# Second stage of a routed two-layer block: rows gathered two experts ahead, whole tiles for large experts, small experts as one chain

## The chip, the cores and the metric

The kernel runs on one core of a Trainium2 chip. The metric is the device time of one execution in microseconds (us), lower is better. Engines are named as in the profile: PE is TensorE's matmul, PEld its weight load, DVE VectorE, ACT ScalarE, POOL GpSimd, SP SyncE. The names with a q behind them (PEldq, POOLq) are the sequencers of these engines: branches, semaphores and the issue of DMAs. L12 is line 12 of the kernel.

## The reference

Three parts follow one another. An attention with rotated queries and keys (4 batches, 8 heads, 576 positions, 64 wide) gives 2304 token rows of 512. A gated layer makes `x = (silu(x @ w_gate) * (x @ w_val)) @ w_out` of them (1536 wide). The third part is a routed layer of 8 experts:

```
do_compute = x @ w_skip > 0                # a token that does not compute keeps its row
xc     = x[do_compute]
logits = xc @ w_gate
e_idx  = argmax(logits)                    # one expert for each token
gate_w = softmax(logits)[e_idx]
y[e]   = gate_w * (relu(xc[e] @ w1[e]) @ w2[e])        # w1: 512x1024, w2: 1024x512
out    = x, and xc + y for the tokens that compute
```

How many rows an expert gets depends on the data; with the inputs used it is 299, 35, 55, 544, 28, 14, 322 and 1 for experts 0 to 7.

## The kernel before

The first two parts end at about 843 us of the span; the change touches what comes then. While the second part runs, each chunk of 384 tokens is routed as soon as it is finished: `note` (L771) writes, for each token that computes, its number, its place in the output and its gate into a list of its expert in a table in DRAM. Expert 0 starts before the last chunk is routed; its first list entries are raised to 128 (`close_first`, L774), which leaves holes, so that its list ends at 335.

`first` runs expert 0's first tile (x00) between the last pieces of the second part, builds the lists of its next two tiles by matmuls (`compare`, `late_list`), gathers their rows (x01, x02), then notes the last chunk and sorts experts 1 to 7 (`sort`): those with more than 64 tokens first. `counts` loads the sorted counts and expert numbers from SBUF into registers of the engines. From here on "expert 1" is the first in the sorted order; here the order is 544, 322, 35, 55, 28, 14, 1.

`run` then loads the index lists (ix, L1367, six tiles of 128 entries for each expert) and the weights. A ring of 21 raw tiles of 512 KB holds weights, eight tiles for an expert (four of w1, four of w2); `w_more(e)` loads what follows when expert e is done. SP issues all of these in program order. POOL issues gathers (L1108) and stores (L1191, L1223); both are indirect DMAs.

An expert with more than 64 rows ("large") is computed in tiles of 128 rows. `ffn` does one: `up` twice (L1141, L1144, one for each half of the 1024 wide middle layer), `turn` twice (L1198, transposes), `down` (L1214 to L1217), `store`. Weights and rows are each split in a high and a low part (eh by ACT at L1071, el by DVE at L1072; `half`), so that each product is three matmuls at a fast rate. The splitting of an expert's weights stands inside its first tile. `mid` transposes the rows of the next tile (`x_T`, L1116) between the two turns. `more` nests the tiles: an `If` per further tile (L1433), each of which gathers the rows of the tile after next.

What is left of an expert behind its whole tiles and is up to 64 rows ("the rest") goes through `few_up`, `few_turn`, `few_down` (L1158 and following), in an `If` of its own: `rest` loads its part of the list (ixrest, L1352, on ACT's queue), `rest_gather` its rows (rest_rows). So a tile starts whole when more than 64 rows are left.

An expert with up to 64 rows ("small") goes through `raw_ffn` in an `If` of its own (L1387), five of these in a row here: gather the next expert's rows, rH for both halves (L1257, the raw weights without a split), the next expert's rows transposed (xTf, L1127), rhT (L1268), Y (L1272), store, `w_more`.

`hint` places a hint of a coming branch on TensorE's sequencer.

Of the kernel before, what the change touches and what calls it, by code (L numbers as in the profile page):

```python
# [7 lines left out]
F32 = mybir.dt.float32  # L8
# [490 lines left out]
class Moe1:  # L499
# [258 lines left out]
    def placed(self, c):  # L758
        nc, k = self.nc, self.k
        pos, row, ps = self.r.pop(c)  # L760
        nc.vector.tensor_tensor(k["run"], k["run"], ps[:, TT * E:(TT + 1) * E], op=ALU.add)
        posu = self.p2.tile([P, TT], U32, tag="rposu", name=f"rposu_{c}")
        nc.vector.tensor_copy(posu, pos)
        self.r[c] = pos, row, posu

# [59 lines left out]
    def sort(self):  # L825
# [17 lines left out]
        nc.vector.tensor_copy(k["n"][0:1, 1:E], pos)  # L843
        nc.vector.tensor_copy(k["n"][0:1, 0:1], nf[:, 0:1])
        nc.vector.tensor_tensor(t, m, col(desc), op=ALU.mult)
        nc.vector.tensor_reduce(pos, t, axis=AX.X, op=ALU.add)
        nc.vector.tensor_scalar(k["n"][0:1, E:], pos, -1.0, float(E), op0=ALU.mult, op1=ALU.add)

    def counts(self):
        load = self.nc.values_load_multi_w_load_instructions  # L850
        n = load(self.k["n"][0:1, 0:E], min_val=0, max_val=NTOK)[1]
        ids = load(self.k["n"][0:1, E:], engines=[mybir.EngineType.SP, mybir.EngineType.Activation], min_val=1, max_val=E - 1)[1]
        return n[0], n[1:], ids
# [83 lines left out]
def load_consts(nc, lasting, c, w, tok, cf, w_gate, w_skip, table):  # L937
# [16 lines left out]
    k["n"] = lasting.tile([P, 2 * E - 1], I32, tag="n", name="n")  # L954
# [24 lines left out]
class Moe2:  # L979
# [4 lines left out]
    def __init__(self, tc, c, w, px, w1, w2, x2d, table, out, ident):  # L984
        self.tc, self.nc, self.w, self.c, self.px = tc, tc.nc, w, c, px
        self.w1, self.w2, self.x2d, self.table, self.out, self.ident = w1, w2, x2d, table, out, ident
        self.W = {}
        self.ring = None
        self.n, self.place, self.pair, self.both = {}, {}, {}, {}
        self.raws = []  # L990
# [9 lines left out]
    def open(self, ctx):  # L1000
        self.fold = self.c.tile([P, FEW], F32, tag="fold", name="fold")
        self.nc.vector.tensor_reduce(self.fold, self.ident.rearrange("p (c a) -> p c a", a=2), axis=AX.X, op=ALU.add)
        self.p1 = ctx.enter_context(self.tc.tile_pool(name="e_1", bufs=1))
        self.fold2 = self.p1.tile([P, FEW], F32, tag="fold2", name="fold2")
        self.nc.vector.tensor_tensor(self.fold2, self.ident[:, :FEW], self.ident[:, FEW:], op=ALU.add)
        self.raws += [self.w.ring.tile([P, F2], I32, tag="raw", name=f"wr{i}") for i in range(4)]
        self.raws.append(self.p1.tile([P, F2], I32, tag="raw2", name="wr4"))
        self.rest_rows = self.p1.tile([P, DM], F32, tag="rest_rows", name="rest_rows")
        self.xf = [self.p1.tile([P, 4 * FEW], F32, tag=f"xf{i}", name=f"xf{i}") for i in range(2)]
        self.xrest = self.p1.tile([P, 2 * DM], F32R, tag="xrest", name="xrest")  # L1010
# [140 lines left out]
    def few_up(self, e, x, fh, work=()):  # L1151

        nc = self.nc
        ps = self.bank("H", f"H{fh}")
        for kt in range(KT):
            for i, w in enumerate(self.w1_of(e, kt, fh)):
                nc.tensor.matmul(ps, x["hl"][:, 2 * kt * P:(2 * kt + 1) * P], w, start=(kt + i == 0),  # L1158
                                 stop=(kt == KT - 1 and i == 1))
        for f in work:  # L1160
            f()
        h = self.w.tmp.tile([P, 512], F32, tag="y2", name=f"h{fh}")
        nc.scalar.copy(h, ps)
        return h

    def few_turn(self, fh, h):

        nc = self.nc
        ps = self.bank("U", f"hT{fh}")[:, :4 * FEW]
        for i in range(4):  # L1170
            nc.tensor.matmul(ps[:, i * FEW:(i + 1) * FEW], h[:, i * P:(i + 1) * P], self.fold, start=True, stop=True)
        ps = ps.rearrange("p (i c) -> p i c", i=4)
        th, tl = self.both[1 - fh][:, :4 * P].rearrange("p (i a c) -> a p i c", i=4, a=2)
        nc.scalar.activation(th, ps, AF.Relu)
        nc.vector.scalar_tensor_tensor(tl, ps, 0.0, f32(th), op0=ALU.max, op1=ALU.subtract)

    def few_down(self, e):
        nc = self.nc
        self.y = self.bank("Y", "Y")
        for n in range(8):  # L1180
            for i, w in enumerate(self.W[1][n // 4]):
                nc.tensor.matmul(self.y, self.both[1 - n // 4][:, n % 4 * P:(n % 4 + 1) * P], w[:, n % 4, :],
                                 start=(n + i == 0), stop=(n == 7 and i == 1))

# [41 lines left out]
    def ffn(self, x, mid=None, few=False, split=None, end=None):  # L1226

        up, turn, down, store = (getattr(self, "few_" * few + f) for f in ("up", "turn", "down", "store"))
# [6 lines left out]
        h0 = up(0, x, 0)  # L1235
        rows(range(0, 3))
        h1 = up(0, x, 1)
        turn(0, h0)
# [3 lines left out]
        turn(1, h1)  # L1242
        rows(range(5, 8))
        if end:
            end()
        down(0)
        store(x)

    def raw_ffn(self, e, x, mid):

        nc = self.nc
        side = lambda ps, a: ps[a * FEW:(a + 1) * FEW]
        hs = []
        for fh in range(2):
            ps = self.bank("H", f"rH{fh}")
            for kt in range(KT):
                nc.tensor.matmul(side(ps, kt % 2), x["f"][:, kt * FEW:(kt + 1) * FEW],  # L1257
                                 self.w.raw[e, kt][:, fh * 512:(fh + 1) * 512],
                                 start=(kt < 2), stop=(kt >= 2), skip_group_check=True)
            h = self.w.tmp.tile([P, 512], F32, tag="y2", name=f"rh{fh}")  # L1260
            nc.scalar.copy(h, ps)
            hs.append(h)
        mid()
        hT = self.w.tmp.tile([P, 8 * FEW], F32, tag="f", name="rhT")
        for fh in range(2):
            ps = self.bank("U", f"rhT{fh}")[:, :4 * FEW]
            for i in range(4):
                nc.tensor.matmul(ps[:, i * FEW:(i + 1) * FEW], hs[fh][:, i * P:(i + 1) * P], self.fold2, start=True, stop=True)  # L1268
            nc.scalar.activation(hT[:, fh * 4 * FEW:(fh + 1) * 4 * FEW], ps, AF.Relu)
        self.y = self.bank("Y", "Y")  # L1270
        for n in range(8):
            nc.tensor.matmul(side(self.y, n % 2), hT[:, n * FEW:(n + 1) * FEW],  # L1272
                             self.w.raw[e, KT + n // 2][:, n % 2 * 512:(n % 2 + 1) * 512],
                             start=(n < 2), stop=(n >= 6), skip_group_check=True)
        self.few_store(x)
# [31 lines left out]
    def first(self):  # L1307
# [40 lines left out]
    def rest(self, base, n, eng):  # L1348

        at = ((n + (P - FEW - 1)) >> 7) << 7  # L1350
        ix = self.p1.tile([P, 1, 3], I32, tag="ixrest", name="ixrest")
        eng.dma_start(ix, self.table[bass.ds(at + base, P)].rearrange("(t p) c -> p t c", p=P))  # L1352
        return ix, at

    def rest_gather(self, ix):
# [173 lines left out]
```

## Time and profile before

| what | us |
|---|---|
| three executions | 1124.89, 1128.54, 1129.74 |
| their median | 1128.54 |
| the profiled execution | 1127.36 |
| its span | 1125.6 |
| PE busy in the span | 996.0 (88%) |
| DVE, ACT, POOL busy | 564.3, 480.8, 442.8 |

The page's slices of 28 us each show PE busy at nine tenths or more through most of the span and at 5 to 7 tenths in most of the last ten slices, where the granted clock of PE (PEclk, tenths of full speed) falls below nine tenths as well:

```
PE   4999989879899999999999999999995679776766
PEclk9999999999899999999999999999996879888787
```

In a row of waits, "xTf <- DMA rows" means that the matmul into xTf waited for the DMA into rows; in a timeline row the bracket holds the engine's idle time before the instruction and what ended it.

### The profile page before, as it was taken

Reading aid. Unit: us, or ns where it says so; the run is one execution under the profiler, and the core shown is the slowest. Engines: PE = TensorE matmul, PEld = TensorE weight load, DVE = VectorE, ACT = ScalarE, POOL = GpSimd, SP = SyncE. Lnnn points to the kernel's source line nnn. Section 1 sums busy time; section 2 is a strip of 40 time slices with the busy share of each in tenths; the row PEclk is TensorE's granted clock in tenths of the full one; section 3 lists DMA queues with packets and bytes.
Section 4 is the critical chain, followed back from the end, with each engine's and each line's share of the span. In section 5 each row is a group of like instructions: output and inputs, shape, how many; then the busy total and the mean of one; then the engine's idle time right before and its main releaser. Section 6 shows DMA issues by size and latency. Waiting matters only on the chain. (4 is left out here: it accounts for less than half of the span.)

```text
span 1125.6 us, 16782 instructions
## 1 busy us (share of the span) xinstructions
PE 996.0 (88%) x5889; PEld 825.0 (73%) x5889; DVE 564.3 (50%) x967; ACT 480.8 (43%) x1043; POOL 442.8 (39%) x442
## 2 busy tenths in 40 slices
PE   4999989879899999999999999999995679776766
PEld 4777767657677888899999999999984468565323
DVE  6777767767667888735433323324532141331011
ACT  4788868767674333323423223124321142330111
POOL 6668777777404445541251331422511111111110
PEclk9999999999899999999999999999996879888787
DMA  5354554554434333224203112122224851141640
GB/s 163 101 136 136 136 141 134 138 147 116 104 99 137 103 107 111 73 76 115 63 8 96 45 41 74 29 84 67 66 74 128 320 194 51 45 174 29 247 152 4
DMA packets 81756, 120.06 MB, mean 107 GB/s; under 512 B 36885, under 2 KB 47781, under 8 KB 81648
## 3 DMA queue, kind: packets, MB, share of 16 engines
q1 hardware_dynamic: 77712, 110.01, 33.1%
q0 software_dynamic: 3504, 8.71, 2.6%
q8 instruction: 54, 0.88, 0.4%
q14 instruction: 54, 0.44, 0.1%
q10 hardware_dynamic: 432, 0.00, 0.0%
HBM read 88.00 MB, written 22.61 MB: 98 GB/s over the span
## 5 line engine op out<-in xcount | busy, mean ns | idle before, releaser
L614 POOL TENSOR_TENSOR hl<-h,hh 128x384 fp32r<-128x384 f32 x72 | 78.5, 1090 | 245.0 <-ACT hh L613 244.9
L251 DVE TENSOR_REDUCE nm<-S 128x1 f32<-128x576 f32 x144 | 108.6, 755 | 45.8 <-PE S L239 44.3
L259 ACT ACTIVATE P<-S,nm 128x576 f32<-128x576 f32 x144 | 107.3, 745 | 3.8 <-DVE nm L251 3.6
L613 ACT CAST hh<-h 128x384 fp32r<-128x384 f32 x72 | 37.0, 514 | 143.0 <-DVE h L612 143.0
L611 DVE TENSOR_TENSOR h<-g,h 128x384 f32<-128x384 f32 x72 | 40.0, 556 | 111.1 <-ACT h L610 111.1
L239 PE MATMUL S<-Bk,Aq 128*128 128x288 f32 x256 | 75.0, 307 | 18.3 <-DMA Bk<-Ak 18.3
L269 PE MATMUL T<-ident,P 128*128 128x128 f32 x576 | 90.8, 281 | 0.0
L627 PE MATMUL Y<-ohi,hh 128*128 128x512 f32 x216 | 87.2, 403 | 0.0
L318 PE MATMUL pv<-pt,rawv 128*64 128x384 f32 (+1 forms) x512 | 85.1, 434 | 1.9 <-ACT pt L284 1.8
L627 PE MATMUL Y<-ohi,hl 128*128 128x512 f32 x216 | 85.8, 397 | 0.7 <-POOL hl L614 0.7
L627 PE MATMUL Y<-olo,hh 128*128 128x512 f32 x216 | 85.4, 395 | 0.0
L239 PE MATMUL S<-Ak,Aq 128*128 128x288 f32 x256 | 82.9, 338 | 1.5 <-ACT P L259 1.5
L604 PE MATMUL g<-xa,ghi 128*128 128x384 f32 x216 | 75.5, 350 | 9.0 <-DVE h L611 8.4
L606 PE MATMUL g<-xa,glo 128*128 128x384 f32 x216 | 72.4, 335 | 0.0
L610 ACT ACTIVATE h<-g 128x384 f32<-128x384 f32 x72 | 35.1, 488 | 87.2 <-PE g L606 83.3
L606 PE MATMUL v<-xa,vlo 128*128 128x384 f32 x216 | 72.2, 334 | 0.0
L604 PE MATMUL v<-xa,vhi 128*128 128x384 f32 x216 | 72.1, 334 | 0.0
L269 PEld LDWEIGHTS T<-ident,P 128*128 128x128 f32 x576 | 64.4, 143 | 2.1 <-issue 1.2
L239 PEld LDWEIGHTS S<-Bk,Aq 128*128 128x128 f32 x256 | 50.8, 198 | 20.5 <-issue 18.4
L612 DVE TENSOR_TENSOR h<-v,h 128x384 f32<-128x384 f32 x72 | 40.2, 558 | 48.0 <-PE v L606 45.3
L239 PEld LDWEIGHTS S<-Ak,Aq 128*128 128x128 f32 x256 | 50.4, 197 | 6.3 <-issue 4.2
L282 DVE COPY pt<-T 128x512 f32<-128x512 f32 x64 | 44.2, 691 | 21.1 <-PE T L269 19.7
(289 smaller groups left out, 2572.1 us busy)
## 6 DMA issues: line engine op xcount, KB each, us to landing
wr_s<-in_moe_w_dram SPq DMA_DIRECT2D x46, 512.0 KB
xT<-x SPq DMA_DIRECT2D x32, 288.0 KB
x<-xT SPq DMA_DIRECT2D x24, 384.0 KB
Bk<-Ak SPq DMA_DIRECT2D x30, 288.0 KB
raw<-in_moe_w_gate_dram SPq DMA_DIRECT2D x12, 512.0 KB
raw<-in_moe_w_val_dram SPq DMA_DIRECT2D x12, 512.0 KB
raw<-in_moe_w_out_dram SPq DMA_DIRECT2D x12, 512.0 KB
wr<-in_moe_w_dram SPq DMA_DIRECT2D x10, 512.0 KB
```

What stands on the lines that cost most here:

```text
L239: nc.tensor.matmul(ps[:, c, :288], l, r[:, c * 288:(c + 1) * 288], start=(j == 0), stop=(j == len(ops) - 1))
L251: nc.vector.tensor_reduce(nm, st_u["S"], axis=AX.XY, op=ALU.max, negate=True)
L259: nc.scalar.activation(pt.rearrange("p (a b) -> p a b", a=2), st_u["S"], AF.Exp, bias=st_u["nm"], scale=1.0, accum_out=self.pairs[p]["l"][ ...
L269: nc.tensor.transpose(ps[:, kt * P:(kt + 1) * P], pt[:, kt * P:(kt + 1) * P], self.ident)
L282: self.nc.vector.tensor_copy(self.pt[:, :, cols], self.units[u]["T"])
L318: nc.tensor.matmul(ps[a * D:a * D + D, :n], st["raw"]["v"][:, h, 2 * third + a], self.pt[:, 2 * third + a, c0:c0 + n], start=(third == 0), ...
L604: nc.tensor.matmul(ps[m], wh[:, kt, cols], xh, start=(kt == 0), stop=False)
L606: nc.tensor.matmul(ps[m], wl[:, kt, cols], xh, start=False, stop=(kt == KT - 1))
L611: nc.vector.tensor_tensor(h, ps["g"], h, op=ALU.mult)
L612: nc.vector.tensor_tensor(h, ps["v"], h, op=ALU.mult)
L614: nc.gpsimd.tensor_tensor(hl, h, f32(hh), op=ALU.subtract)
L627: nc.tensor.matmul(self.acc[c][t], a[:, cols], b, start=(f == 0 and i == 0), stop=(f == FT - 1 and i == 2))
```

## The change

- Tiles start whole whenever any row is left: the thresholds of the tile branches are t\*128 in place of t\*128+64, and `rest`, `rest_gather`, `few_up`, `few_turn`, `few_down` go, with their buffers.
- Rows are gathered two experts ahead: expert e's first rows are gathered at the start of expert e-2 (`rows_of`), a large expert's second rows at the start of expert e-1 (`rows1_of`). Four gathers (first and second rows of expert 1, the fourth tile of expert 0, first rows of expert 2) are issued before the first branch.
- Small experts are a chain: the `Else` arm of `big{e}` holds `few(e)`, which runs e and all experts behind it without a branch, since the sorted order puts the small ones last. In it the next expert's first half of up stands between the turns and the down of the present one, its second half behind the store.
- `first`: `sort` stands ahead of the last down matmuls, `x_T` of x01 ahead of the second list. `count0` loads expert 0's count alone; the other counts are loaded just before the first branch, the expert numbers on SP only.
- Four of the weight loads stand ahead of the ix loads on SP.
- Hints of `big{e+1}` stand in each tile ahead of `down`. The constant `fold` is computed once, at the start.

The core of the diff:

```diff
@@ first
         self.x01 = self.gather(self.x1[0], (self.ix01, gi), 0)
+        m1.sort()
+        self.down(0, range(2, 8))
         m1.compare(1)
-        self.down(0, range(2, 5))
+        self.x_T(self.x01)
         m1.late_list(1, self.ix01, gi)
         self.x02 = self.gather(self.xn[0], (self.ix01, gi), 1)
-        self.down(0, range(5, 8))
-        self.x_T(self.x01)
         self.store(self.x00)
         m1.note(c)
-        m1.sort()
-        return m1.counts()
+        return m1.count0()
@@ run
+        for i in range(KT):
+            self.w_load(1, i)
         for e in range(E):
-            nc.sync.dma_start(ix[e], tiles(slice(0, NI * P) if e == 0 else bass.ds(base[e - 1], NI * P)))
-        for i in range(RING):
+            nc.sync.dma_start(ix[e], tiles(slice(0, NI * P) if e == 0 else bass.ds(self.ids[e - 1] * NTOK, NI * P)))
+        for i in range(KT, RING):
             self.w_load(i // 8 + 1, i % 8)
-        self.first_rows = [None] + [self.gather(self.x0[e], ix[e], 0) for e in (1,)]
-        with tc.If(n0 > P + FEW, label="tile0_1") as cmp:
-            self.hint("tile0_2", n0, 2 * P + FEW)
-            self.ffn(self.x01, mid=lambda: (self.x_T(self.x02), self.x_T(self.first_rows[1], 1)))
-            x3 = self.gather(self.xn[1], ix[0], 3)
+        self.rows_of(1)
+        x3 = self.gather(self.xn[1], ix[0], 3)
+        self.rows1_of(1)
+        self.rows_of(2)
+        self.counts = [None, *self.m1.counts()]
+        with tc.If(n0 > P, label="tile0_1") as cmp:
+            self.hint("tile0_2", n0, 2 * P)
+            self.ffn(self.x01, mid=lambda: (self.x_T(self.x02), self.x_T(self.xs[1], 1)), late=lambda: self.hint_big(1))
...
-        r, at = self.rest(0, n0, nc.scalar)
-        with tc.If(n0 > at):
-            r = self.rest_gather(r)
-            self.x_T(r)
-            self.ffn(r, few=True)
-        self.big(1, n, base, ix)
-        for e in range(1, E):
-            with tc.If(n[e - 1] < FEW + 1):
-                if e + 1 < E:
-                    self.next_rows(e, ix)
-                    self.raw_ffn(e, self.first_rows[e], lambda: self.x_few(self.first_rows[e + 1], (e + 1) % 2))
-                else:
-                    self.raw_ffn(e, self.first_rows[e], lambda: None)
-                self.w_more(e)
+        self.big(1)
@@ big
+        n = self.counts[e]
+        with self.tc.If(n > FEW, label=f"big{e}") as cmp:
+            self.hint(f"tile{e}_1", n, P)
+            self.rows_of(e + 2)
+            x2 = self.gather(self.xn[0], self.ix[e], 2)
+            self.rows1_of(e + 1)
+            def mid():
+                self.x_T(self.xs1[e])
                 if e + 1 < E:
+                    self.x_T(self.xs[e + 1], (e + 1) % 2)
+            self.ffn(self.xs[e], mid, split=e, late=lambda: self.hint_big(e + 1))
+            self.w_more(e)
+            self.more(e, n, self.xs1[e], x2, 1)
             if e + 1 < E:
-                self.next_rows(e, ix)
...
+                self.big(e + 1)
+        with cmp.Else():
+            self.few(e)
+
+    def few(self, e):
+
+        h = [self.raw_up(e, 0), self.raw_up(e, 1)]
+        for e in range(e, E):
+            self.rows_of(e + 2)
+            hT = self.w.tmp.tile([P, 8 * FEW], F32, tag="f", name="rhT")
+            self.raw_turn(0, h[0], hT)
+            if e + 1 < E:
+                self.x_few(self.xs[e + 1], (e + 1) % 2)
+            self.raw_turn(1, h[1], hT)
+            h = [self.raw_up(e + 1, 0)] if e + 1 < E else []
+            self.raw_down(e, hT)
+            self.few_store(self.xs[e])
             self.w_more(e)
+            h += [self.raw_up(e + 1, 1)] if e + 1 < E else []
@@ more
-        with tc.If(n > t * P + FEW, label=f"tile{e}_{t}"):
+        with tc.If(n > t * P, label=f"tile{e}_{t}"):
```

Two places show how the instructions stand. The first is PE among the small experts: xf0 and xf1 are the transposed rows of two experts in turn, wr and wr_s raw weights, rH0 and rH1 the two halves of up, rhT0 and rhT1 the turns. Before, around the end of one small expert and the start of the next:

```order
L1257 MATMUL rH1_15603<-wr_s4_9007,xf0_9387 64x512 x2
L1257 MATMUL rH1_15603<-wr_s5_9008,xf0_9387 64x512 x2
L1127 MATMUL xTf_15610<-ident_66,rows0_8831 128x64 x4
L1268 MATMUL rhT0_15617<-fold2_9379,rh0_15601 128x64 x4
L1268 MATMUL rhT1_15623<-fold2_9379,rh1_15608 128x64 x4
L1272 MATMUL Y_15629<-wr_s6_9009,rhT_15616 64x512 x4
L1272 MATMUL Y_15629<-wr_s7_9010,rhT_15616 64x512 x4
L1387 UNCONDITIONAL_BRANCH x2
L1387 COMPARE_AND_BRANCH
L1257 MATMUL rH0_15655<-wr0_9381,xf1_9388 64x512
```

and now, in the arm that the sorted order enters with its third expert:

```order
L1230 MATMUL rhT0_15265<-fold_4564,rh0_15254 128x64 x4
L1128 MATMUL xTf_15271<-ident_66,rows0_8833 128x64 x4
L1230 MATMUL rhT1_15277<-fold_4564,rh1_15261 128x64 x4
L1219 MATMUL rH0_15283<-wr_s1_8827,xf0_9256 64x512
L1219 MATMUL rH0_15283<-wr_s2_8884,xf0_9256 64x512 x2
L1219 MATMUL rH0_15283<-wr_s3_8885,xf0_9256 64x512
L1236 MATMUL Y_15290<-wr4_9255,rhT_15264 64x512 x2
L1236 MATMUL Y_15290<-wr_s0_8826,rhT_15264 64x512 x4
L1236 MATMUL Y_15290<-wr_s1_8827,rhT_15264 64x512 x2
L1219 MATMUL rH1_15314<-wr_s1_8827,xf0_9256 64x512
```

The branches between the experts are gone, the transposes of the next rows stand between the two turns, and the first half of the next up (rH0) ahead of Y.

The second place is POOL between the note of the last chunk (table) and the first tile branches; n is the tile of counts, gi0, gi1 and gi2 are the row numbers of expert 0, 1 and 2. Before:

```order
L771 DMA table_65<-rrow_5_9085,rposu_5_9135 19200x3 x3
L851 TENSOR_LOAD n_5772
L1108 DMA rows0_8831<-x2d_64,gi1_9429 128x512
L1372 COMPARE_AND_BRANCH
L1223 DMA out_0_dram<-o_9534,ix01_9123 2304x512
L1108 DMA rows1_8984<-x2d_64,gi0_9427 128x512
L1433 COMPARE_AND_BRANCH
```

and now:

```order
L773 DMA table_65<-rrow_5_9087,rposu_5_9137 19200x3 x3
L851 TENSOR_LOAD n_5774
L1109 DMA rows0_8833<-x2d_64,gi1_9361 128x512
L1109 DMA rows1_8986<-x2d_64,gi0_9359 128x512
L1109 DMA rows1_8986<-x2d_64,gi1_9361 128x512
L1109 DMA rows0_8833<-x2d_64,gi2_9363 128x512
L858 TENSOR_LOAD n_5774
L1329 COMPARE_AND_BRANCH
L1190 DMA out_0_dram<-o_9542,ix01_9125 2304x512
L1399 COMPARE_AND_BRANCH
```

The gather of expert 0's fourth tile (gi0) moved from behind the store of the second tile to ahead of the first branch, and two gathers of experts 1 and 2 came to stand there too.

## Rows read from the trace of the kernel before

**Rows 1.** Windows of the second stage; columns as in the first line.

```profile
core 0: us, PE busy (x) PEld busy (x) DVE busy (x) ACT busy (x) POOL busy (x), PEclk, DMA share, GB/s
...
892.40:925.30 32.90, 18.24 (x68) 14.69 (x69) 13.94 (x23) 12.56 (x24) 5.06 (x5) 0.74 0.59 198
925.30:963.10 37.80, 37.80 (x181) 31.04 (x180) 7.92 (x12) 8.03 (x15) 5.97 (x6) 1.00 0.14 43
963.10:973.90 10.80, 9.69 (x49) 7.87 (x48) 1.60 (x3) 1.94 (x4) 1.01 (x1) 1.00 0.07 25
973.90:1004.20 30.30, 17.38 (x69) 13.95 (x69) 14.57 (x24) 13.15 (x25) 5.10 (x5) 0.77 0.55 177
...
1029.40:1038.90 9.50, 0.14 (x1) 0.02 (x1) 0.75 (x1) 0.00 (x0) 1.01 (x1) 0.78 0.10 26
1038.90:1116.70 77.80, 60.04 (x256) 28.98 (x256) 5.71 (x8) 13.43 (x28) 7.62 (x8) 0.79 0.41 146
1116.70:1125.60 8.90, 0.00 (x0) 0.00 (x0) 1.43 (x2) 0.58 (x1) 0.92 (x1) 0.69 0.01 1
...
1050.00:1056.00 6.00, 4.90 (x24) 1.44 (x20) 1.43 (x2) 1.76 (x3) 1.82 (x2) 1.00 1.01 392
1044.00:1050.00 6.00, 6.00 (x36) 3.31 (x34) 0.00 (x0) 1.63 (x4) 0.00 (x0) 0.92 0.75 247
```

**Rows 2.** PE's waits, 843 to 1126: waited for, us in total, times, longest.

```profile
PE xTf L1127 <- DMA rows<-x2d,gi: 17.7, 3, 6.9
PE H L1141 <- ACT eh L1071: 13.6, 2, 7.6
PE xT L1116 <- DMA rows<-x2d,gi: 11.6, 2, 8.4
...
PE xT L1116 <- DMA rest_rows<-x2d,girest: 7.0, 1, 7.0
```

**Rows 3.** Timeline, 845 to 870: start us, us, engine, line, operation, count, idle before.

```profile
857.33 4.57 SPq L1367 DMA_DIRECT2D ix<-table  x8
...
861.36 0.99 POOL L1108 DMA_INDIRECT rows<-x2d,gi  x1 [6.18 <-DVE gi L1100]
...
866.33 1.08 PE L1116 MATMUL xT<-ident,rows 128*128 128x128 f32 x4 [8.38 <-DMA rows<-x2d,gi]
```

**Rows 4.** Timeline of PE, a third tile of expert 0 and a covered tile.

```profile
880.42 0.60 PE L1198 MATMUL hT<-ident,h 128*128 128x128 f32 x4
...
930.93 0.60 PE L1198 MATMUL hT<-ident,h 128*128 128x128 f32 x4
...
937.91 0.39 PE L1141 MATMUL H<-eh,xhl 128*128 128x512 f32 x1
```

**Rows 5.** Timeline, start of the first large expert.

```profile
899.35 4.26 ACT L1071 CAST eh<-wr_s 128x512 fp32r<-128x512 f32 x8 [12.75 <-DMA out_dram<-o,ix]
...
900.00 4.95 DVE L1072 TENSOR_TENSOR el<-wr_s,eh 128x512 fp32r<-128x512 f32 x8 [6.83 <-ACT eh L1071]
```

**Rows 6.** Branches by line, ns min/median/max, first/last start; last row: 1020 to 1035.

```profile
L1433 PEldq COMPARE_BRANCH  x12: 65/127/6356, 870.6 to 1029.7; - x12
...
L1403 PEldq COMPARE_BRANCH  x4: 72/138/3225, 895.9 to 1034.5; - x4
...
L1387 PEldq COMPARE_BRANCH  x12: 65/174/2617, 1034.8 to 1113.6; - x12
...
L1387 POOLq INC_SWDGE_SEM  x2: 1107/1118/1128, 1038.5 to 1039.9; - x2
...
L1433 PEldq COMPARE_BRANCH  x2: 186/1832/3478, 1025.7 to 1029.7; - x2
```

**Rows 7.** Timeline among the small experts: a gather and its use, then one expert's matmuls.

```profile
1055.12 0.97 POOL L1108 DMA_INDIRECT rows<-x2d,gi  x1 [0.30 <-DMA wr_s<-in_moe_w_dram]
...
1061.64 0.66 PE L1127 MATMUL xTf<-ident,rows 64*128 64x64 f32 x4 [6.73 <-DMA rows<-x2d,gi]
...
1107.57 3.60 PE L1257 MATMUL rH<-wr_s,xf 128*64 128x512 f32 x16
...
1111.10 2.00 PE L1268 MATMUL rhT<-fold,rh 128*128 128x64 f32 x16
...
1113.03 3.65 PE L1272 MATMUL Y<-wr_s,rhT 128*64 128x512 f32 x16
```

More of the change, by code (lines that the diff above doesn't have):

```diff
@@ L989, in __init__ @@
         self.n, self.place, self.pair, self.both = {}, {}, {}, {}
+        self.fold = c.tile([P, FEW], F32, tag="fold", name="fold")
+        self.nc.vector.tensor_tensor(self.fold, ident[:, :FEW], ident[:, FEW:], op=ALU.add)
         self.raws = []
@@ L1149, in up @@
         return h
[L1151 to L1183, printed above, removed]
     def few_store(self, x):
@@ L1224, in store, with ffn @@
                                      bounds_check=NTOK - 1, oob_is_err=False)
-    def ffn(self, x, mid=None, few=False, split=None, end=None):
-        up, turn, down, store = (getattr(self, "few_" * few + f) for f in ("up", "turn", "down", "store"))
+    def ffn(self, x, mid=None, split=None, late=None):
         half = (lambda ns, k: [self.half(split, i, k) for i in ns]) if split is not None else lambda ns, k: None
@@ L1241, in ffn @@
             mid()
-        turn(1, h1)
+        self.turn(1, h1)
         rows(range(5, 8))
[L1244 to L1269, printed above, removed]
@@ new lines, in ffn, with raw_up @@
+        if late:
+            late()
+        self.down(0)
+        self.store(x)
+    def raw_up(self, e, fh):
+        ps = self.bank("H", f"rH{fh}")
+        for kt in range(KT):
+            self.nc.tensor.matmul(ps[kt % 2 * FEW:(kt % 2 + 1) * FEW], self.xf[e % 2][:, kt * FEW:(kt + 1) * FEW],
+                                  self.w.raw[e, kt][:, fh * 512:(fh + 1) * 512],
+                                  start=(kt < 2), stop=(kt >= 2), skip_group_check=True)
+        h = self.w.tmp.tile([P, 512], F32, tag="y2", name=f"rh{fh}")
+        self.nc.scalar.copy(h, ps)
+        return h
@@ L1346, in w_splits, with run @@
                 self.w_load(0, i + 4)
[L1348 to L1355, printed above, removed]
-        return self.gather((self.rest_rows, self.xrest), (ix, self.numbers(ix, self.p1, "rest")), 0)
-    def run(self, n0, n, ids):
+    def run(self, n0):
@@ L1395, in next_rows @@
-    def next_rows(self, e, ix):
-        x = self.gather(self.x0[(e + 1) % 6], ix[e + 1], 0)
-        if e + 1 == len(self.first_rows):
-            self.first_rows.append(x)
-    def big(self, e, n, base, ix):
-        count = n[e - 1]
-        with self.tc.If(count > FEW, label=f"big{e}"):
-            self.hint(f"tile{e}_1", count, P + FEW)
-            r, at = self.rest(base[e - 1], count, self.nc.scalar)
-            x1 = self.gather(self.x1[e % 2], ix[e], 1)
-            if e + 1 < E:
-                self.next_rows(e, ix)
-            x2 = self.gather(self.xn[0], ix[e], 2)
-            rows = []
-            def after():
-                rows.append(self.rest_gather(r))
-                self.x_T(x1)
-                if e + 1 < E:
-                    self.x_T(self.first_rows[e + 1], (e + 1) % 2)
-            self.ffn(self.first_rows[e], after, split=e, end=lambda: self.x_T(rows[0]))
-            self.w_more(e)
-            self.more(e, count, ix[e], x1, x2, 1)
-            if e + 1 < E:
-                self.hint(f"big{e + 1}", n[e], FEW)
-            with self.tc.If(count > at):
-                self.ffn(rows[0], few=True)
-            if e + 1 < E:
-                self.big(e + 1, n, base, ix)
@@ new lines, in run, with rows_of, rows1_of, hint_big @@
+        with cmp.Else():
+            self.x_T(self.xs[1], 1)
+        self.big(1)
+    def rows_of(self, e):
+        if e < E:
+            x = self.gather(self.x0[e % 6], self.ix[e], 0)
+            if e == len(self.xs):
+                self.xs.append(x)
+    def rows1_of(self, e):
+        if e < E:
+            x = self.gather(self.x1[e % 2], self.ix[e], 1)
+            if e == len(self.xs1):
+                self.xs1.append(x)
+    def hint_big(self, e):
+        if e < E:
+            self.hint(f"big{e}", self.counts[e], FEW)
@@ L1493, in build @@
     m2.open(ctx)
-    m2.run(*n)
+    m2.run(n)
 EARLY = 4
```

71 lines of the change are left out of this document (36 added, 35 removed).

## The prediction

> **What bounds the kernel now.** I read the page first, then a table of windows, then TensorE's waits, then the timeline around each wait. The diff touches only the second stage, from about 843 us of the 1125.6 us span to its end. In the windows [rows 1] the stage falls into pieces of two kinds. Whole tiles behind one another keep PE busy throughout: 37.80 of 37.80 us, clock 1.00. Every start of something new does not: 18.24 of 32.90 us where the first large expert begins, 17.38 of 30.30 where the second does, 0.14 of 9.50 ahead of the small experts. So the stage is bound by what PE waits for at each start, and the waits [rows 2] name it: 17.7 us in three waits of xTf (the next small expert's rows), 13.6 in two of H (the first split weights of a large expert), 11.6 for gathered rows, 7.0 for the rest's rows. Each stretch after such a wait also runs at a lower granted clock: 0.74 and 0.77 in the large experts' starts, 0.79 among the small ones.
>
> The inputs give the counts that the branches see. Expert 0 has 299 tokens, and its list has holes up to 335; the two large ones have 544 and 322, the five small ones 35, 55, 28, 14 and 1. Thresholds of t\*128 in place of t\*128+64 leave expert 0 and the 322 with the three tiles each that they run now; the 544 goes from four tiles and a rest of 32 to five tiles.
>
> **The change part by part**, along PE's path, after minus before.
>
> 1. Front, up to the first large expert's rows. Sort and count come earlier, but PE then waited 8.38 us for rows [rows 3]: SP's eight ix loads (from 857.33) follow the list's notes, the gather starts at 861.36, the matmul at 866.33. The earlier sort does not shorten that chain; the second list now stands behind the down matmuls, so the notes shift later by about half a microsecond, and four weight loads, 512 KB each, stand ahead of the ix loads on SP (their issue is short, and the ix loads waited anyway). Between the time that the front's earlier start could give (2 us of the 8.38) and four loads' transfer at 392 GB/s (1.3 us each, [rows 1]; 5 us), I take +0.7, near the lower end because the ix loads wait for the notes, not for SP. Bounds -2 to +5.
>
> 2. Expert 0's third tile. Its turn starts at 880.42 and its expert ends at 892.40, 11.98 us; the same piece of a covered tile goes from 930.93 to 937.91, 6.98 us [rows 4]. The difference is the fourth tile's gather, issued only inside the branch; it is now issued ahead of the first branch. -5.0, bounds -5.2 to -2.
>
> 3. First large expert's start, 32.90 us. Two delays stand in it. ACT's casts begin only at 899.35, behind ACT's load of the rest's list, which waits for a store to the output; and 7.0 us go to the rest's gather [rows 2, 5]. With `rest` gone, ACT is free at 892.4. What is then late is the split itself: eight ACT casts and eight DVE subtractions take 4.95 us [rows 5], 0.62 each. Branches and the last store of expert 0 (about 1.5 us), eight subtractions (5.0) and the four last up matmuls bring the first half to about 8 us after the expert's start; from the end of that half to the tile's end a further 9 to 10 us, as a covered tile has (6.98 of it from its turn on). So 17.7, or -15.2. If the split's start stays late by a branch fetch (6.36 us, [rows 6]) it is -8.8; bounds -18 to -7.
>
> 4. The rest of 32 rows, 10.80 us, becomes a whole tile of 12.60 (37.80/3) [rows 1]: +1.8, bounds 1.0 to 2.5.
>
> 5. Second large expert's start, 30.30 us [rows 1], is the same picture, with the wait for casts 6.0 (13.6 less 7.6, [rows 2]): 30.3 to 16.9, -13.4, bounds -16 to -6.
>
> 6. Ahead of the small experts, 9.50 us with PE idle. TensorE's sequencer stood in three branches there, 3.48, 3.23 and 2.62 us [rows 6]. One far jump (big's Else) remains, at about 3.2, with its hint moved ahead of down: 3.5 in all, -6.0. Bounds -8.5 (all hinted in time) to 0 (as many fetches as now).
>
> 7. Small experts, 77.80 us [rows 1]. At full clock one takes 3.60 (rH) + 2.00 (rhT) + 3.65 (Y) [rows 7], and xTf at most 0.66: some 9.6 each. Now it is 77.8/5 = 15.6, as each step's gather is issued in that step and lands 6.5 us after it (issued at 1055.12, used at 1061.64). In the chain a step's gather is for the expert after next. POOL's order there is store of e-1, then gather of e+2, and an INC_SWDGE_SEM of 1.1 us [rows 6] may stand before each: store (1.1 and about 1), INC (1.1), gather to use 6.5. Counted from the end of the Y before, with DVE's output ahead, that is about 11 us, and the rows are wanted about 12.4 us after it (the up half of 1.8, one step of 9.6, half a turn of 1.0). It fits with some 1.5 us to spare. The next expert's up half, put between the turn and Y, hides ACT's copies. Nineteen weight tiles of 512 KB are left at that point; at 392 GB/s [rows 1] 25 us, in a chain of 48. First step 4.5 (cold up), four of 9.6, and the last of 5.8: 48.7, -29.1. Bounds: nothing hidden but the branches (5 x 0.2 and one of the waits, 6.7) -8; nothing exposed and the first step at full clock -31.
>
> The tail behind the last matmul, 8.9 us [rows 1], stays: the last expert's output still goes Y, DVE, POOL store.
>
> Here a rule speaks against the change. The Trainium skill ("Runtime: NRT & Kernel Launch", Instruction fetch mechanics) says that a taken branch to a target outside the window being held forces a fetch before anything executes, and that the prefetch is purely sequential. The trace agrees that some jumps cost 2.6 to 6.4 us and others 0.07 [rows 6]. By that rule code repeated in seven arms buys nothing where the arm is first entered; it would leave step 6 at 9.5, and the sum 6 us less.
>
> Sum: +0.7 -5.0 -15.2 +1.8 -13.4 -6.0 -29.1 = -66.2. The profiled execution took 1127.36 us (span 1125.6, 1.76 around it), 1.2 below the median of the runs shown. 1127.36 - 66.2 = 1061.2; with the 1.2, **1062 us**.
>
> **Rivals.**
>
> A. *Jumps.* Code is longer in the nest and the branches at tile0_3, tile1_5, tile2_3 and big3 are all taken to far targets. For: the rows of 6.36, 3.23 and 2.62 us, with hints present before as well. Against: the medians of the groups are 0.13 to 0.17 us, and a fetch under the wait for casts was hidden. Price: one of 6.4 in step 3 and 3.5 more in step 6, +10: 1072.
>
> B. *Small experts stay bound by rows or weights.* For: landing 6.5 us plus POOL's INCs leaves 1.5 us. If three gathers are late by 3 us each and the weights run at 247 GB/s, the other rate in the small experts' windows [rows 1] (2.1 us a tile, 40 us for 19, of which some 4 show), +13: 1075; with half of the waits and of the low clock left, +15 (half of 29.1): 1077. Against: the order of POOL's rows, two experts ahead.
>
> C. *The waits come back under other names.* If every start has another thing as late as the one removed (casts behind stores, rows behind notes, fetches in place of gathers), only terms 1 and 4 are left, +2.5, and a few branches saved: about 1128, no change. For: terms 3, 5 and 7 each suppose that what is next late is early enough. Against: three different mechanisms would have to fail together.
>
> D. *TensorE at half clock*, the slower side. The shorter waits might not keep the clock at its upper level; small experts' matmuls of 64 rows with copies between could leave it at 1.2 GHz. What is left of PE work at full rate is ten tiles of 12.6 and five experts of 9.4, 173 us, and each microsecond of it at half clock costs another. Beyond 66/173 = 38% the gain is gone; with two thirds at half clock, +115, 1062 + 115 = 1177. For: the windows of the starts show 0.74 to 0.79 now, and the second small expert's turn and Y were slow behind the wait. Against: the stretch of whole tiles has 1.00, and the low clock followed an idle stretch each time.
>
> **How the numbers follow.** Forecast 0.60, A 0.15, B 0.18, C 0.03, D 0.03, the rest to a better case (all lower bounds of terms 3, 5 and 7 together, -7.3: 1055). The range takes the forecast with its terms' smaller errors (about 8 either way), A and B whole: 1051 to 1083. A measurement of this kernel cannot tell a change under 0.5%, 5.6 us. Faster by more than that holds in all cases but C and D: 0.95; within it 0.02; slower 0.03.
>
> **What would show it right or wrong.** In the profile after: no wait on an `ixrest` load or a rest's rows; the first large expert's casts starting within 2 us of expert 0's last matmul; each covered tile 12.6 us; in the chain xTf without waits for rows, and steps of 9.6; PE idle ahead of the chain under 5 us. If steps of the chain are still 12 us or more with xTf waiting on rows, B is it; if TensorE's sequencer is named ahead of H or rH with more than 5 us, A; if the granted clock in the tiles is near 0.5 with PE busy, D. The forecast is wrong where the sum of terms 3, 5 and 7 comes to less than 45 us.

## The result, and the profile after

The changed kernel takes 1064.82 us (median of 1063.37, 1064.82 and 1068.54), against 1128.54 before: ratio 0.9449, 95% interval 0.9398 to 0.95. A second series of five gave 1063.53 and 0.9445 (0.9428 to 0.9461). The forecast was 1062 with a range of 1051 to 1083. The profiled execution's span is 1066.7 us, 58.9 less than before, where the terms summed to 66.2. Of all executions in this document two stood far off the others, one of 2052.32 us of the kernel before and one of 1239.36 us of an experiment, and they are in no ratio and no median.

Windows of the changed kernel, cut where PE's pieces of work end; columns as in [rows 1]:

```profile
843.60:868.60 25.00, 8.35 (x33) 6.59 (x32) 2.90 (x13) 2.30 (x5) 7.81 (x8) 0.68 0.49 122
868.60:877.00 8.40, 8.35 (x32) 7.14 (x33) 2.75 (x5) 1.48 (x3) 0.95 (x1) 0.75 0.99 346
877.00:889.60 12.60, 12.60 (x61) 10.22 (x59) 2.64 (x4) 2.67 (x5) 1.99 (x2) 1.00 1.04 398
889.60:911.70 22.10, 17.12 (x66) 12.61 (x66) 13.14 (x21) 11.97 (x23) 4.77 (x4) 0.85 0.82 304
911.70:962.00 50.30, 50.30 (x241) 41.45 (x239) 10.56 (x16) 10.71 (x20) 6.97 (x7) 1.00 0.16 51
962.00:980.60 18.60, 16.03 (x66) 11.64 (x66) 13.19 (x21) 11.96 (x23) 4.41 (x4) 0.91 0.71 234
980.60:1005.80 25.20, 25.20 (x121) 20.63 (x119) 5.27 (x8) 5.35 (x10) 3.97 (x4) 1.00 0.23 73
1005.80:1008.90 3.10, 0.13 (x3) 0.07 (x3) 0.75 (x1) 0.00 (x0) 1.01 (x1) 1.00 0.13 41
1008.90:1057.80 48.90, 48.74 (x256) 22.04 (x256) 5.71 (x8) 13.36 (x28) 6.65 (x7) 0.97 0.62 229
1057.80:1066.70 8.90, 0.05 (x2) 0.00 (x0) 1.43 (x2) 0.58 (x1) 0.91 (x1) 0.66 0.02 4
```

Read against [rows 1], each row answers a term. Starts of large experts last 22.1 and 18.6 us (32.9 and 30.3 before), the gap ahead of the small experts 3.1 (9.5), the small experts 48.9 (77.8) at a granted clock of 0.97 (0.79), and PE is busy in all but 0.2 us of them.

PE's waits in the same stage, against [rows 2]; waited for, us in total, times, longest:

```profile
PE xT L1117 <- DMA rows<-x2d,gi: 15.6, 1, 15.6
PE H L1142 <- ACT eh L1072: 4.8, 2, 3.9
PE rH L1219 <- issue: 3.1, 2, 3.0
PE Y L1181 <- ACT pair L1167: 1.5, 2, 0.7
```

The waits for xTf and the rest's rows are gone, those for the casts are a third. One wait grew: the first large expert's rows, 15.6 us in one piece where it was 8.4. Its end moved by only 2.3 us, though; the rest is that PE came to it 4.9 us earlier (853.07 instead of 857.95), since this wait for VectorE in expert 0's second tile, before the change, is gone:

```profile
PE H L1141 <- DVE fold L1002: 5.5, 1, 5.5
```

| term | predicted | measured |
|---|---|---|
| 1 front, to those rows | +0.7 | +2.3 (868.65 less 866.33, [rows 3]) |
| 2 expert 0's last two pieces | -5.0 | -5.1 |
| 3 first large expert's start | -15.2 | -10.8 |
| 4 rest becomes a tile | +1.8 | +1.7 |
| 5 second large expert's start | -13.4 | -11.7 |
| 6 gap ahead of the small experts | -6.0 | -6.4 |
| 7 small experts | -29.1 | -28.9 |
| sum | -66.2 | -58.9 |

Terms 1, 3 and 5 miss by 7.7 us together. What happened in the first two can be read in the timeline of the changed kernel: POOL's gather of x01 and three notes, the matmul on the first large expert's rows, and ACT's casts for that expert.

```profile
838.92 0.98 POOL L1109 DMA_INDIRECT rows<-x2d,gi  x1 [16.94 <-DVE sort L840]
...
847.52 1.00 POOL L773 DMA_INDIRECT table<-rrow,rposu  x1 [0.30 <-issue]
854.86 0.97 POOL L773 DMA_INDIRECT table<-rrow,rposu  x1 [6.33 <-DMA table<-rrow,rposu]
858.17 0.97 POOL L773 DMA_INDIRECT table<-rrow,rposu  x1 [2.34 <-DMA table<-rrow,rposu]
...
868.65 1.08 PE L1117 MATMUL xT<-ident,rows 128*128 128x128 f32 x4 [15.58 <-DMA rows<-x2d,gi]
...
893.03 4.26 ACT L1072 CAST eh<-wr_s 128x512 fp32r<-128x512 f32 x8 [8.08 <-PEq L1399]
```

The tile branches of the same kernel on TensorE's sequencer; ns min/median/max, first and last start:

```profile
L1399 PEldq COMPARE_BRANCH  x13: 65/77/6959, 873.7 to 1006.1; - x13
```

The second note left 7.3 us after the first. The casts were released by PE's sequencer (PEq), which stood 6.96 us, from 885.92, in the branch past expert 0's third tile, until 3.3 us beyond the end of the last matmul at 889.6.

### The profile page after: what moved, and what is told of

It reads as the page before. It is cut to its first block, busy times and chain, and to the rows that moved or that the text cites. A ratio compares the mean times of both kernels' runs of the same rounds, so it can differ in the third digit from the quotient of the medians.

```text
span 1066.7 us, 16446 instructions
## 1 busy us (share of the span) xinstructions
PE 984.9 (92%) x5893; PEld 816.7 (77%) x5893; DVE 559.4 (52%) x962; ACT 479.5 (45%) x1041; POOL 442.6 (41%) x441
```

## The experiments

Twelve kernels ran in three series; the kernel before ran beside each of them (medians 1126.14, 1126.26 and 1125.93), and each ratio is to it. The place of the stage in a profile varies by itself: the gather of x01, which stands ahead of every edit of the experiments, starts anywhere from 833.0 to 839.5 us in the fourteen profiles. So where times in single profiles are compared below, they are counted from that gather, which before the change is

```profile
839.46 0.98 POOL L1108 DMA_INDIRECT rows<-x2d,gi  x1 [16.94 <-DVE rm L809]
```

**Weights back behind the ix loads.**

```diff
-        for i in range(KT):
-            self.w_load(1, i)
         for e in range(E):
             nc.sync.dma_start(ix[e], ...)
-        for i in range(KT, RING):
+        for i in range(RING):
             self.w_load(i // 8 + 1, i % 8)
```

> The changed kernel with the four weight loads put back behind the eight ix loads on SP; nothing else. Theory: the 2 MB that they move lie in front of the last chunk's notes (second note 7.3 us after the first, where it was 2.9 us before the change), so the notes close up to about 3 us apart, the first large expert's rows come about 4 us earlier (matmul at about 864.7 instead of 868.65) and the time falls from 1064.8 to about 1061. Rival: the notes are late because the second list, its gather and the store stand ahead of them on POOL; then the gap stays near 7 us and the time within 1 us of 1064.8.

1058.99 us, ratio 0.9411 (0.936 to 0.9463), where the changed kernel has 0.9449 and 0.9445: by the time alone not clear of it. The timeline is clearer:

```profile
835.71 0.97 POOL L1109 DMA_INDIRECT rows<-x2d,gi  x1 [16.93 <-DVE sort L840]
...
844.20 1.00 POOL L773 DMA_INDIRECT table<-rrow,rposu  x1 [0.30 <-issue]
846.87 0.97 POOL L773 DMA_INDIRECT table<-rrow,rposu  x1 [1.67 <-DMA table<-rrow,rposu]
849.87 0.97 POOL L773 DMA_INDIRECT table<-rrow,rposu  x1 [2.03 <-DMA table<-rrow,rposu]
...
860.12 1.09 PE L1117 MATMUL xT<-ident,rows 128*128 128x128 f32 x4 [10.38 <-DMA rows<-x2d,gi]
```

The gap of the first two notes is 2.7 us and PE's wait 10.4. From the gather of x01 to this matmul it is 24.4 us; 29.7 and 29.0 in the two profiles of the changed kernel, 26.9 before the change. Only the place of the four loads differs, so they delayed the notes, and the rival is out.

**Notes first, too.**

```diff
         m1.compare(1)
+        m1.note(c)
         self.x_T(self.x01)
         m1.late_list(1, self.ix01, gi)
         self.x02 = self.gather(self.xn[0], (self.ix01, gi), 1)
         self.store(self.x00)
-        m1.note(c)
```

> As the kernel before it in this list, and the last chunk's three notes are issued ahead of the gather of expert 0's third tile and of the first tile's store on POOL. Theory: the chain notes, ix loads, gather, matmul sets the end of the front, and nothing but POOL's order holds the first note until 847.5; notes from about 840, ix loads at about 850, rows at about 858, so PE's wait falls from 15.6 us to about 6, less a wait of some 3 us for the third tile's rows, which are now later: about 1055. Rival: the notes take as long wherever they start, since each waits for the one before (6 us each beside other traffic): gain of 3 us at most over the run before it, about 1059.

1055.76 us, ratio 0.9365 (0.931 to 0.942). The notes started at 838.71 and were 2.8 us apart; the waits for rows:

```profile
PE xT L1117 <- DMA rows<-x2d,gi: 6.5, 3, 4.6
```

The 15.6 us have become 4.6, and the third tile's rows are late by 1.5, not 3. From the gather of x01 (837.43) to the matmul on the first large expert's rows (856.21) it is 18.8 us, 5.6 less than in the run before it, where 6 had been expected. By the medians only 3 us were gained from that run, and the intervals of the two overlap.

**The chain with rows one ahead.**

```diff
         for e in range(e, E):
-            self.rows_of(e + 2)
+            self.rows_of(e + 1)
```

> The changed kernel, but inside the chain of small experts each step gathers the rows of the next expert and not of the one after it (the first of these repeats a gather already made). Theory: the rows two experts ahead carry term 7; waits for rows of about 6 us come back in the later steps with half-clock turns and Y after them, steps of 14 to 16 us, +18 to +24, about 1085. Rival: the chain without branches and with the next up inside the step carries it; then it is +3 at most, under 1068.

1098.49 us, ratio 0.9779 (0.9714 to 0.9843): some 35 us of the gain are lost, more than the theory's 18 to 24. The wait for the next small expert's rows:

```profile
PE xTf L1128 <- DMA rows<-x2d,gi: 21.3, 4, 7.8
```

The window of its small experts:

```profile
1005.00:1086.60 81.60, 60.25 (x256) 26.98 (x256) 5.71 (x8) 13.50 (x28) 7.60 (x8) 0.80 0.40 140
```

81.6 us, longer than the 77.8 of before. 21.3 us are waits; PE's busy time is 11.5 us more than the changed kernel's 48.74 for the same 256 matmuls, at a clock of 0.80 where it has 0.97. The expectation took too little for the second part. One reason why it comes out behind the old branches can be read in the order: between store and next rows PE has half an up and half a turn here, where before it had a whole up, and the longest wait is 7.8 us instead of 6.9. What two experts ahead are worth by themselves is read from the kernel before with that part alone, further below.

**The chain without interleaving.**

```diff
-            h = [self.raw_up(e + 1, 0)] if e + 1 < E else []
             self.raw_down(e, hT)
             self.few_store(self.xs[e])
             self.w_more(e)
-            h += [self.raw_up(e + 1, 1)] if e + 1 < E else []
+            h = [self.raw_up(e + 1, 0), self.raw_up(e + 1, 1)] if e + 1 < E else []
```

> The changed kernel, but in the chain both halves of the next expert's up stand behind the down and store of the present one. Theory: the up between turn and down only hides ACT's copy of the turned rows and of the up's second half, some 0.7 to 1.4 us a step: +4 to +7, about 1070. Rival: it is worth nothing since PE's queue covers it (within 1 us), or much more (+12 and more) since each gap costs a stretch of half clock as well.

1063.78 us, ratio 0.9449 (0.9403 to 0.9495): no difference. My theory was wrong here, and the rival that PE's queue covers it holds:

```profile
1006.70:1055.30 48.60, 48.52 (x256) 22.14 (x256) 5.71 (x8) 13.34 (x28) 6.63 (x7) 0.97 0.62 229
```

PE is idle for 0.1 us of it: ACT's copies lie under the next rows' transposes and the other half's turn anyway.

**Later weights.** Loads 8 to 20 wait on SP for the output of expert 0's third tile:

```diff
+        self.o = o
...
-        for i in range(KT, RING):
+        for i in range(KT, 8):
             self.w_load(i // 8 + 1, i % 8)
...
                 self.ffn(x, mid=..., late=...)
+                if (e, t) == (0, 2):
+                    last = self.p1.tile([1, 4], F32, tag="last", name="last")
+                    self.nc.sync.dma_start(last, self.o[0:1, 0:4])
...
+        for i in range(8, RING):
+            self.w_load(i // 8 + 1, i % 8)
         self.big(1)
```

> The changed kernel, but of the 21 weight loads only the eight of the first large expert are issued ahead of expert 0's tiles; the 13 others wait on SP for the output of expert 0's third tile (by a 16-byte copy of it). Theory: the branch past expert 0's third tile (6.96 us at 885.92, the casts wait for it until 893.03) takes so long because its code comes in beside weight transfers at 390 to 410 GB/s; with the queue empty it takes about 3.5 us as the branch at 1002.07 does, ends under the matmuls, and the casts start at about 889.8: -3 to -5, about 1060.5. Rival: the target is as far as before and the fetch stays at 6 to 7 us: within 1 us of the changed kernel; or the later weights are missed by the second large expert or the small ones, which costs 2 us and more.

1061.75 us, ratio 0.943 (0.9397 to 0.9463). By itself the time is not clear of the changed kernel's; the trace is. Its tile branches:

```profile
L1402 PEldq COMPARE_BRANCH  x13: 65/77/4114, 869.7 to 998.2; - x13
```

The casts of the first large expert in its timeline:

```profile
885.84 4.26 ACT L1072 CAST eh<-wr_s 128x512 fp32r<-128x512 f32 x8 [5.22 <-PEq L1402]
```

The window of its longest branch:

```profile
881.60:885.70 4.10, 3.81 (x17) 2.82 (x15) 0.25 (x1) 0.00 (x0) 0.00 (x0) 1.00 0.03 4
```

With 4 GB/s on the queues the same jump takes 4.11 us; in the changed kernel it took 6.96, at 389 GB/s (885.9 to 892.9). PE's longest wait for the casts falls from 3.9 to 1.1 us, and the first large expert's start takes 18.6 us (885.26 to 903.86) instead of 22.1, or 20.7 in the second profile of the changed kernel. The later weights are missed nowhere: PE's weight loads wait for them 0.3 us in three places, as in the changed kernel.

**Single parts of the change, on the kernel before.** Whole tiles and no rest (thresholds t\*128, `rest` and the few_ tiles taken out):

```diff
-        with tc.If(n > t * P + FEW, label=f"tile{e}_{t}"):
+        with tc.If(n > t * P, label=f"tile{e}_{t}"):
...
-            r, at = self.rest(base[e - 1], count, self.nc.scalar)
...
-                rows.append(self.rest_gather(r))
...
```

> The kernel before with one part of the change: tile thresholds of t*128 and no rest (its loads, gathers and few_ tiles are gone); rows are gathered as before. Theory: terms 3 to 5 are due to this part alone: the casts of the large experts start behind expert 0's branch (about 3.5 us after its last matmul) and not behind the rest's list, no wait for the rest's rows, one more whole tile: -10.8 + 1.7 - 11.7 = -20.8, and one branch fewer ahead of the small experts, 0 to -3: ratio about 0.98. Rival: second rows gathered only at the start of an expert take the place of the rest's rows, and half of the two starts' waits stays: -10.

1103.82 us, -22.4, ratio 0.9794 (0.9759 to 0.9829). The casts' waits fall from 13.6 in two to 3.9:

```profile
PE H L1141 <- ACT eh L1071: 3.9, 2, 3.0
```

The rows' waits do not fall (17.6 in four), since this kernel gathers second rows in the expert itself: the rival is there with two waits of 4.1 and 2.5 us, one in each start, but not with half. The gap ahead of the small experts stays, too:

```profile
PE rH L1257 <- DMA out_dram<-o,ix: 8.7, 1, 8.7
```

The fourth tile's gather early:

```diff
+        x3 = self.gather(self.xn[1], ix[0], 3)
         with tc.If(n0 > P + FEW, label="tile0_1") as cmp:
             self.ffn(self.x01, mid=...)
-            x3 = self.gather(self.xn[1], ix[0], 3)
```

> The kernel before with the gather of expert 0's fourth tile issued ahead of the first branch, nothing else. Theory: the 3.2 us wait in expert 0's third tile and its half-clock turns go: third tile 12.6 us instead of 17.6, -5, ratio about 0.9955. Rival: the casts of the first large expert wait for ACT's list load behind the output store anyway, whose landing sets that start; then the 5 us return as a longer wait there and the time stays within 1 us.

1123.97 us, ratio 0.9983 (0.996 to 1.0006): not told apart from no change, and the theory's 0.9955 lies just outside. The wait for rows in the third tile is gone, and this one is longer than the 7.6 of [rows 2]:

```profile
PE H L1141 <- ACT eh L1071: 16.5, 2, 10.5
```

2.9 us of the 5 come back as a longer wait for the list load behind the output store. In the changed kernel, where no list load stands there, the same piece is shorter by 5.1 us and that wait is gone; no run has these two parts together and nothing else.

Rows two experts ahead, in the old branches:

```diff
-        self.first_rows = [None] + [self.gather(self.x0[e], ix[e], 0) for e in (1,)]
+        self.first_rows = [None] + [self.gather(self.x0[e], ix[e], 0) for e in (1, 2)]
...
-        x = self.gather(self.x0[(e + 1) % 6], ix[e + 1], 0)
+        x = self.gather(self.x0[(e + 2) % 6], ix[e + 2], 0)
...
```

> The kernel before with the first rows of an expert gathered two experts ahead (two before the first branch, then one in each expert, large or small), nothing else: the small experts stay in their branches and their order of work. Theory: rows two ahead are all of term 7; no wait for xTf, steps of about 10 us, 77.8 us becomes 50 to 53, ratio about 0.977. Rival: without the chain, branches and PE's fetches in them keep each step at 12 us or more, and half of the gain is missing: 62 us, ratio about 0.986.

1093.21 us, -33.0, ratio 0.9704 (0.9674 to 0.9734), some 7 us more than expected. The small experts, and the gap ahead of them:

```profile
1032.20:1082.20 50.00, 49.69 (x256) 23.04 (x256) 5.70 (x8) 13.00 (x28) 6.63 (x7) 0.94 0.60 222
1022.80:1032.20 9.40, 0.06 (x1) 0.01 (x1) 0.75 (x1) 0.00 (x0) 1.01 (x1) 0.78 0.08 25
```

50.0 us with every branch still in place, 48.9 in the chain: 27.8 us of the gain are here, as expected. Of the 34.5 us between the profiled executions 4.3 stand ahead of the gather of x01 (835.21 against 839.46), where the edit changes nothing. Since the order inside the steps is worth nothing (the chain without interleaving), the branches between small experts cost 1 us in all. What the `Else` arm saves is the gap: 9.4 us here and 8.7 without the rest, 3.1 in the changed kernel. No run has that arm alone.

**Both repairs together, hints, and the place of the third note.**

> The changed kernel unchanged, as the base for the kernels beside it: ratio 0.943 to 0.947.

> The two repairs together: weights behind the ix loads and the notes ahead of the third tile's gather (1055.8 when run with the early weights all at once), and 13 of the 21 weight loads held back until expert 0's third tile is out (-3 by itself). Theory: the two act at different places, front and first large expert's start, so they add: about 1052.5, ratio to before about 0.934. Rival: with the front shorter by 12 us the fetch and the weights of the first large expert come closer together, so the branch past the third tile again takes over 6 us and nothing is added: 1055.5, 0.937.

1048.12 us, ratio 0.932 (0.9296 to 0.9345), against 0.9445 (0.9428 to 0.9461) of the changed kernel beside it: 15.4 us less. The theory's 0.934 lies in the interval, the rival's 0.937 does not. Its waits for rows and casts, and its tile branches, without one of over 6 us:

```profile
PE xT L1117 <- DMA rows<-x2d,gi: 6.2, 3, 4.7
...
PE H L1142 <- ACT eh L1072: 1.9, 2, 1.1
...
L1400 PEldq COMPARE_BRANCH  x13: 65/77/4094, 858.6 to 985.8; - x13
```

The gather of x01 in the changed kernel beside it (span 1062.4), then in this one (span 1046.3):

```profile
837.84 0.97 POOL L1109 DMA_INDIRECT rows<-x2d,gi  x1 [16.95 <-DVE sort L840]
...
833.72 0.97 POOL L1109 DMA_INDIRECT rows<-x2d,gi  x1 [16.94 <-DVE sort L840]
```

From there to the end it is 224.6 and 212.6 us: the stage is 12.0 shorter, where the theory had 12.3. So the two repairs add. The other 4.1 us between these two profiles stand ahead of the gather, where no edit is; their cause is open.

```diff
     def hint(self, label, n, least):
+        return
```

> The changed kernel without any branch hint on TensorE. Theory: the jumps that are taken to far targets cost 3 to 7 us with the hint or without it (rows of 6.96, 3.53 and 2.30 us in the changed kernel, all hinted), so the hints are worth at most the branches into the next tile or expert, which are the fall-through: within 2 us of the changed kernel. Rival: the hints are what makes the ten other branches 0.07 to 0.4 us; without them each entry into a tile fetches 2.5 us and more, part of it exposed: +8 or more.

1065.67 us, ratio 0.9467 (0.9445 to 0.9489), intervals overlapping with the changed kernel's. The branches without hints:

```profile
L1399 PEldq COMPARE_BRANCH  x13: 65/65/6257, 868.2 to 997.6; - x13
...
L1359 PEldq COMPARE_BRANCH  x4: 65/1854/4064, 887.3 to 1048.8; - x4
```

Entries into tiles stay at 0.065 us and far jumps at 3.4 to 6.3: the medians lie 2 us apart, and the rival's 8 us and more are out. The jump to the small experts took 4.06 instead of 2.30 (2.70 in the second profile), the only row that moved against it.

```diff
-        m1.note(c)
+        m1.note(c, (0, 1))
         self.x_T(self.x01)
         m1.late_list(1, self.ix01, gi)
         self.x02 = self.gather(self.xn[0], (self.ix01, gi), 1)
+        m1.note(c, (2,))
...
```

> As the kernel with both repairs, but the third note stands behind the gather of expert 0's third tile instead of ahead of it: POOL waits for the second note's landing there in any case. Theory: the third tile's rows land about 1.3 us earlier and its wait of 1.5 us goes, while the third note is at most 1 us later: within 1 us of it. Rival: the gather stands between the notes as it did in the changed kernel and the notes lose its 1.3 us and more: +1 to +3.

1052.0 us, ratio 0.9341 (0.9322 to 0.936). The third tile's wait is gone (4.8 us in two waits, 6.2 in three), but its interval overlaps with the one of the two repairs: not told apart.

## Why the prediction was right, and where its terms were off

Terms 2, 4, 6 and 7 came out within half a microsecond. For term 7, the largest, the two experiments from both sides show the cause: rows two ahead alone give it on the kernel before (50.0 us), and without them the chain is at 81.6. The count of POOL's store, gather and landing up to the need was right in what it decided: no xTf waited. What was to spare is not quite the 1.5 us counted. The chain's last two gathers were issued 8.4 and 8.5 us ahead of their use (1025.93 to 1034.35, 1035.31 to 1043.83); against the 6.5 us of [rows 7] that leaves some 2 us, an estimate, and no INC_SWDGE_SEM stood between store and gather there. The sentence that the interleaved up "hides ACT's copies" was not right: there is nothing to hide.

Term 6 came out by a reading that was not quite right. Of the three branches that it counts in the gap the first, 3.48 us at 1025.7 [rows 6], was over before the gap began at 1029.4; two stood in it, and one is left, of 2.30 us.

Term 1 was mis-sized (+0.7, measured +2.3) by its own choice of end: the bound of five microseconds for "four loads' transfer" was named and set aside "because the ix loads wait for the notes, not for SP". That is so, but the notes are DMAs themselves and lay behind the weights. The error was to ask which queue the ix loads stand in and not what else moves while the notes land. The term took a value between its two bounds, where both happened and added up: from the gather of x01 the front alone is 2.5 us shorter than before (24.4 against 26.9), and the weights add 4.6 to 5.3.

Term 3 (-15.2, measured -10.8) carries rival A's mechanism in part: the case of a start late by a branch fetch, priced at 6.36 us and given as -8.8, happened, with 3.4 us from the last matmul to the casts where the term had 1.5. The prediction's own sign, casts within 2 us, failed here and held for the second large expert (0.3 us). It is the same branch that [rows 6] show with 6.36; before, it lay under the wait for ACT's list load. Taking that wait away uncovered it. Of the four branches that rival A named, two more took long, 3.53 us (hidden) and 2.30; the one past the first large expert's last tile, at 962.4, took 0.18.

The other half of the miss of term 3, and that of term 5 (-13.4, measured -11.7), stands behind the turn. From there to the tile's end both terms took the 6.98 us of a covered tile. In the two starts of the changed kernel it is 9.2: from the first of these lines to the window's end at 911.70, and from the second to the last.

```profile
902.50 0.60 PE L1165 MATMUL hT<-ident,h 128*128 128x128 f32 x4
...
971.38 0.60 PE L1165 MATMUL hT<-ident,h 128*128 128x128 f32 x4
...
976.78 0.50 PE L1181 MATMUL Y<-eh,pair 128*128 128x512 f32 x1 [0.73 <-ACT pair L1167]
...
978.11 0.50 PE L1182 MATMUL Y<-el,pair 128*128 128x512 f32 x1 [0.30 <-DVE el L1073]
...
980.59 0.39 PE L1142 MATMUL H<-eh,xhl 128*128 128x512 f32 x1
```

The split of the expert's second weights goes on there on ACT and DVE, PE waits for both, and it transposes the rows of two tiles where a covered tile transposes one; how the 2.2 us divide was not taken apart. The granted clock is not it: it is 1.00 in both stretches. The lower clock of the two windows (0.85 and 0.91) falls ahead of the turn. There the second start took 9.4 us, less than the 9.9 that its 16.9 left for it, and the first, with the late casts, 12.9 instead of 10.7.

The time came nearer to the forecast (2.8 us) than the profile to the sum (7.3), and part of that is luck: the profiled execution was the slowest of its three, 3.7 us above their median. In the second profile the span is 63.2 us shorter than before.

Rivals B, C and D did not occur. D would have had to show in the windows: of those in which PE is busy throughout, one is at 0.75 (868.60 to 877.00, behind the long wait), the others at 0.97 and more.

On fetches the Trainium skill ("Runtime: NRT & Kernel Launch", Instruction fetch mechanics) had been weighed as leaving term 6 at 9.5 us. It came to 3.1. The trace agrees with the rule in that far jumps still cost 2.3 to 7 us. What it does not decide is how many are exposed: one of 3.53 us ran under the matmuls at 1002.07, one of 2.30 did not. The Trainium skill calls the fetch a DMA there, and the jump's 6.96 us beside weights and 4.11 us without agree with that.

## What to carry to other kernels

Gather rows as many steps ahead as issue and landing take against one step; here a step takes 9.5 us, store, gather and landing were counted at about 11, and the second step ahead decided 28 us among the small experts, while branches between the steps and the order inside them decided 1. When a wait is removed, look for what ran hidden beneath it: the fetch of a far jump was there in the profile of before and became the next bound. And before bulk transfers are put early because their queue is free, look for a chain of small DMAs that starts then: here 2 MB of weights delayed such a chain by about 5 us.

## What the runs showed of the hardware that was not expected

A small indirect DMA (128 rows of 12 bytes) let the next one go 2.7 to 4.1 us after its issue where no weights were loaded just ahead, and 7.0 to 7.3 us in the six profiles with 2 MB of weights issued 0.4 to 3.5 us ahead of it. The far jump past expert 0's third tile took 6.1 to 7.0 us on TensorE's sequencer in every kernel that loaded its weights beside it, and 4.1 to 4.5 in the three that held them back. Removing every branch hint moved the time by no more than the measurement can tell (ratios 0.9467 and 0.9445).
